# A three-stage float32 kernel (attention, then two expert layers) on one core: late attention's weights times values in unsplit float32, two heads side by side, with a new order of the work

## The chip, the core and the metric

The kernel runs on one core of a Trainium2 chip. The core has five engines that run side by side, each through its own list of instructions in order: TensorE (PE; its weight loads are shown as PEld), VectorE (DVE), ScalarE (ACT), GpSimd (POOL) and SyncE (SP), whose queue issues nearly all transfers. The metric is the device time of one execution in microseconds (us); lower is better.

## What is computed

The reference, cut to what matters:

```python
# attention: 4 batches, 8 heads, 576 positions, head size 64
scores = scale * np.matmul(q, k.transpose(0, 1, 3, 2))
bias = -(cum[:, :, :, None] - cum[:, :, None, :])       # cum: running sum of max(s, 0)
scores = np.where(causal, -1000000000.0, scores + np.minimum(bias, 0.0))
attn = np.exp(scores - np.max(scores, axis=-1, keepdims=True))
attn = attn / (np.sum(attn, axis=-1, keepdims=True) + 1e-09)
attn_out = np.matmul(attn, v)
x = attn_out.transpose(0, 2, 1, 3).reshape(2304, 512)
# two layers, each 512 -> 2048 -> 512
h = x @ moe_w_in;  x = (h * np.clip(h + 3.0, 0.0, 6.0) / 6.0) @ moe_w_out
h = x @ moe2_w_in; x = (h * np.tanh(softplus(h))) @ moe2_w_out
```

All tensors are float32, and the weights of the layers arrive as 64-bit words.

## The kernel before

**Attention** is cut into two kinds of work, each for a pair of heads. `small` (16 of them) does the first 256 query positions of a pair, `unit` (16) the other 320 against all 576 keys; the change's name "late attention" means the units. Each makes scores on PE, a masked sum with the row's extreme on DVE, the exponential on ACT, a normalisation, and PE transposes of the weights into PSUM banks, which are moved into a tile `pt`. Then PE multiplies weights and values (PV).

**float32 by parts.** A product that must keep float32's precision is made of float32r matmuls: each operand is split into a high part (a copy into float32r) and a low part (a subtraction on DVE), and three or four products of the parts are added in PSUM. `split` and the last steps of `load_split` are such splits. The small units' PV (L685) takes plain float32 operands instead, without parts, and puts one head's 64 output rows in the lower half of the PSUM bank and the other head's in the upper half. A unit's PV (L576) is split: `vt` holds the high and low part of v side by side, 128 columns for one head, `pt` holds both parts of the weights (L559 makes the low ones), each head has a bank `po` and ten matmuls, and the bank's two halves are added at L580 (ACT) and L582 (DVE) into a tile `x`, which is stored in DRAM as `xs`.

**The layers** go over five blocks of tokens (512, 512, 384, 512, 384), and in each block over 16 steps of 128 hidden columns. A step is a first product (L736, four groups of three matmuls, one group for each quarter of the inner dimension), a nonlinearity on ACT and DVE with a split into the tile `g` or `wo`, and a second product (L769 in the first layer, L774 in the second), which gathers in four banks over the 16 steps and is evicted by `y_out` (L792). The first layer's blocks 0 and 1 are written by the small units straight from PSUM (L695 writes the low part); blocks 2 to 4 are loaded from `xs` by `load_block` and split there. Block i's quarter c needs the heads 2c and 2c + 1 of all its batches.

**The order** is made by a list planner (`Plan.run`) while the program is built. Every piece of work has an engine or a choice of two, a guessed cost, a priority and the buffers it needs; the planner takes the ready piece of the lowest priority, and the resulting list of each engine is fixed. The priorities come from offsets in the table `T`. `la` and `la2` say by how many steps the first products go ahead of the second ones in the first and second layer. Buffers rotate in rings: `st`, from which x and y are stored, has four.

Of the kernel before, what the change touches and what calls it, by code (L numbers as in the profile page):

```python
# [34 lines left out]
    sm=4.004, sm2=3.667, w0=5.919, w1=9.193, cum=14.045, wo=0.795, blk0=27.645, blk1=17.49, wo2=40.913,  # L35
    wo2r=11.978, win2=5.088, g=29.605, upre=6.511, uhalf=0.883, upost=2.212, uv=0.304, spre=9.559, shalf=0.728,
    spost=1.761, pe=4.796, bias=2.278, la=1, la2=1, wp=5.083, p0=-8.796, p1=2.0, p2=2.856,
    p3=60.483, p4=83.372, p5=119.475, s0=31.523, s1=22.0, s2=23.277, s3=50.368, s4=66.006, s5=29.106,
# [207 lines left out]
def tile_attention_moe_moe(ctx, tc, qk1, qk, v1, s, w_in, w_out, w2_in, w2_out, out):  # L246
    nc = tc.nc

    def r(ap):
# [4 lines left out]
        "wo": 3, "qk": 2, "cb": 2, "nm": 2, "l": 2, "v": 1, "pt": 1, "qkr": 2,  # L254
# [22 lines left out]
    xs = [[dr.tile([P, n], F32, name=f"xs{i}_{c}") for c in range(NCC)] for i, (_, n) in enumerate(BLOCKS)]  # L277
# [18 lines left out]
    setup_b = Buf(dyn("att"), "pt", [P, 3 * S + CTOT], F32)  # L296

    def rows():
        room = setup_b.t[0:NB * NH]
        s_sb, one, cum = (room[:, S * i:S * (i + 1)] for i in range(3))  # L300
        return s_sb, one, cum, room[:, 3 * S:3 * S + CTOT]
# [121 lines left out]
    def unit(b, h, prio, step, dep0, depc, banks):  # L423
# [94 lines left out]
        pt = Buf(ap, "pt", [P, 2, 2, 1280], F32R)  # L518
        prev_t = None
        n_p = []  # L520
        for i in range(ta, tb):
# [9 lines left out]
            for g, cs in ([(0, (4, 3)), (0, (2, 1, 0))] if i == 4 else [(0, range(i, -1, -1)), (1, range(i, -1, -1))]):  # L531
# [9 lines left out]
                def views(ps, cs, i, g):  # L541
                    nch = len(cs)
                    if i == 4:
                        s_ = ps.t[:, 0:nch * P].rearrange("p (c g n) -> p c g n", g=2, n=D)
                        z0, st = (0, 4) if cs[0] == 4 else (9, 5)
                        d = [pt.t[:, k].rearrange("p g (c n) -> p c g n", n=D)[:, z0:z0 + st * (nch - 1) + 1:st] for k in range(2)]
                    else:
                        s_ = ps.t[:, 0:nch * P].rearrange("p (c n) -> p c n", n=P)
                        qo = P * i - q0
                        d = [pt.t[:, k, g].rearrange("p (c n) -> p c n", n=nq)[:, 4 - nch:, qo:qo + P] for k in range(2)]  # L550
                    return s_, d[0], d[1]
# [12 lines left out]
        x = Buf(main_p, "st", [P, 512], F32)  # L564
        n_x, n_pv = [], None
        for g in range(2):
            po = Bank(banks)
            hi, lo = (0, D) if g == 0 else (D, 0)

            def pv(po=po, g=g):  # L570
                for c in range(tb):
                    a = max(0, P * c - q0)
                    f = (3 - c) * nq + a if c < 4 else 0
                    w = vt.t[:, g, c].rearrange("p a d -> p (a d)")
                    for k in range(2):
# [366 lines left out]
```

## Time and profile before

| | us |
|---|---|
| median of 3 runs | 1014.72 (1013.29 to 1015.25) |
| the profiled execution | 1013.87 |
| its span | 1012.1 |
| PE busy | 992.1 |
| DVE busy | 541.8 |
| ACT busy | 496.0 |

The span runs from the first instruction's start to the last one's end; the execution's own time is 1.77 us longer. Busy times of PE overlap between neighbouring matmuls, so what a matmul takes of PE's time is read from its start to the next one's start. Attention's last matmul of a unit lies near 471 us; what follows is layers alone.

### The profile page before, as it was taken

What the parts mean: (1) busy time and instruction counts of PE and PEld (TensorE: products, weight loads), DVE (VectorE), ACT (ScalarE), POOL (GpSimd) and SP (SyncE); (2) the same over time, 40 slices, a digit from 0 to 9 for tenths busy, and PEclk for the clock granted to TensorE, in tenths of its full rate; (3) what the DMA queues carried; (4) which work ended last, traced back from release to release, by engine and by line L of the source; (5) the groups of instructions that cost most, each with busy time, mean ns of one, the idle gap of its engine ahead of it and who ended that gap; (6) DMA issues with size and microseconds to landing.
All of it is one profiled execution on the core that took longest, in us unless ns stands there. A gap on an engine that the chain in (4) does not pass through costs nothing.

```text
span 1012.1 us, 13938 instructions
## 1 busy us (share of the span) xinstructions
PE 992.1 (98%) x5016; PEld 826.6 (82%) x5016; DVE 541.8 (54%) x1213; ACT 496.0 (49%) x1046; POOL 45.0 (4%) x102
## 2 busy tenths in 40 slices
PE   6999999999999999999999999999999999999997
PEld 3557777778787898988889998888888888888896
DVE  6888988877767776774627888612112112111111
ACT  4878777756555666665326456423223223222222
POOL 2111101110010000000000000000000000000000
PEclk9889999999999999999999999999999999999999
DMA  6767857785565756543526775201001102000101
GB/s 215 231 211 259 287 190 246 227 284 178 171 186 169 238 176 197 177 123 137 207 104 237 261 266 201 86 1 53 22 1 42 42 1 63 0 1 1 42 1 32
DMA packets 56900, 140.81 MB, mean 139 GB/s; under 512 B 6944, under 2 KB 20288, under 8 KB 56832
## 3 DMA queue, kind: packets, MB, share of 16 engines
q1 hardware_dynamic: 56832, 139.93, 42.5%
q8 instruction: 40, 0.66, 0.3%
q14 instruction: 28, 0.23, 0.1%
HBM read 119.22 MB, written 20.68 MB: 138 GB/s over the span
## 4 chain that ended last, share of the span: by engine, by line
PE 89%; DVE 2%; DMA 2%; ACT 2%; issue 0%; DVEq 0%; ACTq 0%; SPq 0%
PE b L736 38%; PE b L774 20%; PE b L769 19%; PE b L492 4%; PE b L576 3%; PE b L538 3%; PE b L631 1%; DMA ys<-st 1%; PE b L685 1%; PE b L676 1%; DMA xs<-st 0%; ACT cb L527 0%; DVE pt L559 0%; DMA blk<-xs 0%; DMA cb<-cums 0%
## 5 line engine op out<-in xcount | busy, mean ns | idle before, releaser
L736 PE MATMUL b<-blk,win 128*128 128x512 f32 (+1 forms) x1920 | 504.4, 374 | 2.8 <-DVE e L749 1.2
L736 PEld LDWEIGHTS b<-blk,win 128*128 128x128 f32 x1920 | 348.9, 189 | 61.8 <-issue 5.7
L769 PE MATMUL b<-g,wo 128*128 128x512 f32 (+1 forms) x960 | 259.1, 380 | 0.1
L769 PEld LDWEIGHTS b<-g,wo 128*128 128x128 f32 x960 | 168.5, 188 | 27.8 <-issue 10.5
L757 DVE TENSOR_TENSOR g<-e,g 128x512 fp32r<-128x512 f32 (+1 forms) x120 | 76.6, 638 | 183.6 <-ACT g L290 183.0
L754 ACT ACTIVATE e<-b 128x512 f32<-128x512 f32 (+1 forms) x80 | 44.4, 555 | 254.2 <-PE b L736 253.5
L774 PE MATMUL b<-wo,g 128*128 128x512 f32 x432 | 122.1, 392 | 0.4 <-ACT g L290 0.4
L774 PE MATMUL b<-wo,wo 128*128 128x512 f32 x432 | 122.2, 391 | 0.0
L757 DVE TENSOR_TENSOR wo<-e,wo 128x512 fp32r<-128x512 f32 (+1 forms) x40 | 25.5, 638 | 136.1 <-ACT wo L290 136.1
L290 ACT ACTIVATE g<-e 128x512 fp32r<-128x512 f32 (+1 forms) x103 | 60.5, 587 | 65.6 <-PE b L769 52.5
L774 PEld LDWEIGHTS b<-wo,g 128*128 128x128 f32 x432 | 80.4, 188 | 13.9 <-ACT g L290 0.9
L774 PEld LDWEIGHTS b<-wo,wo 128*128 128x128 f32 x432 | 80.7, 188 | 12.7
L747 ACT ACTIVATE e<-b,three 128x512 f32<-128x512 f32 (+1 forms) x80 | 51.3, 642 | 34.8 <-PE b L736 22.4
L507 ACT ACTIVATE cb<-cb,nm 128x384 f32<-128x384 f32 (+2 forms) x80 | 54.5, 683 | 26.2 <-DVE nm L499 26.0
L559 DVE TENSOR_TENSOR pt<-b,pt 128x384 fp32r<-128x384 f32 (+2 forms) x96 | 54.6, 577 | 15.2 <-ACT pt L290 14.2
L749 DVE SCALAR_TENSOR_TENSOR e<-e,b 128x512 f32<-128x512 f32 (+1 forms) x80 | 50.4, 630 | 19.0 <-ACT e L747 18.6
L290 ACT ACTIVATE pt<-b 128x384 fp32r<-128x384 f32 (+2 forms) x96 | 48.1, 505 | 24.9 <-PE b L538 24.1
L499 DVE CUSTOM_DVE_ANT_0 cb<-b,cb 128x384 f32<-128x384 f32 (+2 forms) x80 | 44.7, 588 | 17.2 <-PE b L492 15.2
L538 PE MATMUL b<-ident,cb 128*128 128x128 f32 x304 | 48.7, 273 | 0.6 <-DVE pt L559 0.4
L538 PEld LDWEIGHTS b<-ident,cb 128*128 128x128 f32 x304 | 38.3, 140 | 12.2 <-issue 2.2
L576 PEld LDWEIGHTS b<-pt,v 128*128 128x128 f32 x320 | 46.8, 189 | 1.7
L492 PE MATMUL b<-qk 64*128 64x384 f32 (+2 forms) x288 | 46.5, 364 | 0.6 <-DVE pt L559 0.6
(83 smaller groups left out, 862.2 us busy)
## 6 DMA issues: line engine op xcount, KB each, us to landing
wo<-wos SPq DMA_DIRECT2D x64, 512.0 KB, 3.9
wraw<-in_w_in_dram SPq DMA_DIRECT2D x32, 512.0 KB, 4.4
wraw<-in_w_out_dram SPq DMA_DIRECT2D x32, 512.0 KB, 4.4
cb<-cuml SPq DMA_DIRECT2D x16, 896.0 KB, 7.0
wos<-wo SPq DMA_DIRECT2D x16, 512.0 KB, 5.7
qkr<-in_qk_dram SPq DMA_DIRECT2D x16, 480.0 KB, 3.8
qkr<-in_v_dram SPq DMA_DIRECT2D x16, 320.0 KB, 6.7
cb<-cums SPq DMA_DIRECT2D x12, 384.0 KB, 4.3
```

The costliest lines, as they stand in the source:

```text
L290: nc.scalar.activation(out=out_, in_=in_, func=AF.Copy)
L492: nc.tensor.matmul(out=ps[g].t[:, 0:w], lhsT=t.t[s_, ka, qo:qo + P], rhs=t.t[s_, kb, nk0 + a:nk0 + e], start=k == 0, stop=k == 2)
L507: nc.scalar.activation(out=p.t[:, o:o + w], in_=p.t[:, o:o + w], func=AF.Exp, scale=-1.0, bias=nm.t[:, k:k + 1], accum_out=l.t[:, k:k + 1],)
L538: nc.tensor.transpose(out=ps.t[:, P * z:P * (z + 1)], in_=p.t[:, o:o + P], identity=ident)
L559: nc.vector.tensor_tensor(out=dl, in0=s_, in1=r(dh), op=ALU.subtract)
L576: nc.tensor.matmul(out=po.t[:, a:nq], lhsT=w, rhs=pt.t[:, k, g, f:f + nq - a], start=c == 0 and k == 0, stop=c == tb - 1 and k == 1)
L736: nc.tensor.matmul(out=hps.t[:, 0:N], lhsT=w.t[:, a, P * c:P * (c + 1)], rhs=x.t[:, c, b, :], start=(c == 0 and k == 0), stop=(c == NCC - ...
L747: a = add("ACT", actp(N, 1), lambda: nc.scalar.activation(out=e0.t[:, 0:N], in_=hps.t[:, 0:N], func=AF.Relu, bias=three, scale=1.0), [prev ...
L749: a = add("DVE", v1x(N), lambda: nc.vector.scalar_tensor_tensor(out=e0.t[:, 0:N], in0=e0.t[:, 0:N], scalar=6.0, in1=hps.t[:, 0:N], op0=ALU ...
L757: gl = add("DVE", v1x(N), lambda: nc.vector.tensor_tensor(out=g.t[:, 1, 0:N], in0=src.t[:, 0:N], in1=r(g.t[:, 0, 0:N]), op=ALU.subtract), ...
L769: nc.tensor.matmul(out=y[j].t[:, 0:N], lhsT=wt.t[:, a, P * j:P * (j + 1)], rhs=g.t[:, b, 0:N], start=(f == 0 and k == 0), stop=(f == NF - ...
L774: nc.tensor.matmul(out=y[j].t, lhsT=g.t[:, a, P * j:P * (j + 1)], rhs=wt.t[:, b, :], start=(f == 0 and k == 0), stop=(f == NF - 1 and k == 2),
```

## The change

A unit's v is loaded as float32 into a tile of its own and not split. `pt` holds each weight once, as float32; L559 and its 96 subtractions are gone, and the eviction may go to ACT or DVE. PV becomes one group of ten float32 matmuls, over the five key chunks and in each over the two heads, whose outputs lie in the two halves of one bank. The output is split as it leaves that bank: a high part `xh` (copy) and a low part `xl` (subtraction on DVE), both stored, so that `xs` has two halves and `load_block` of the first layer loads them without a split. `v` and `pt` have two buffers each. All offsets of the order are new, `la` goes from 1 to 3 and `la2` from 1 to 2.

```diff
-    spost=1.761, pe=4.796, bias=2.278, la=1, la2=1, wp=5.083, p0=-8.796, p1=2.0, p2=2.856,
...
+    spost=1.158, pe=5.322, bias=2.302, la=3, la2=2, wp=11.079, p0=-8.796, p1=2.0, p2=2.856,
...
-        "wo": 3, "qk": 2, "cb": 2, "nm": 2, "l": 2, "v": 1, "pt": 1, "qkr": 2,
+        "wo": 3, "qk": 2, "cb": 2, "nm": 2, "l": 2, "v": 2, "pt": 2, "qkr": 2,
...
-    xs = [[dr.tile([P, n], F32, name=f"xs{i}_{c}") for c in range(NCC)] for i, (_, n) in enumerate(BLOCKS)]
+    xs = [[dr.tile([P, 2, n], F32, name=f"xs{i}_{c}") for c in range(NCC)] for i, (_, n) in enumerate(BLOCKS)]
...
-        vt = Buf(ap, "v", [P, 2, tb, 2, D], F32R)
-
-        def v_view(low):
-            return vt.t[:, :, :, low, :]
-        vr = Buf(ap, "qkr", [P, 2, tb, D], F32)
-        n_v0 = A("SP", 0.5, lambda: nc.sync.dma_start(
-            out=vr.t, in_=v1[b, h:h + 2].rearrange("g p c d -> p g c d")), dep0, prio, [vr], lat=dma(P * 2 * tb * D * 4))
-        n_v1 = A(("ACT", "DVE"), (act(2 * tb * D), v2x(2 * tb * D)), lambda e: copy(e, v_view(0), vr.t), [n_v0], prio + T["uv"] * step, [vt], [vr])
-        n_v2 = A("DVE", v1x(2 * tb * D), lambda: nc.vector.tensor_tensor(
-            out=v_view(1), in0=vr.t, in1=r(v_view(0)), op=ALU.subtract), [n_v1], prio + T["uv"] * step, (), [vt, vr])
+        vt = Buf(ap, "v", [P, 2, tb, D], F32)
+        n_v = A("SP", 0.5, lambda: nc.sync.dma_start(
+            out=vt.t, in_=v1[b, h:h + 2].rearrange("g p c d -> p g c d")), dep0, prio + T["uv"] * step, [vt], lat=dma(P * 2 * tb * D * 4))
...
-        pt = Buf(ap, "pt", [P, 2, 2, 1280], F32R)
+        pt = Buf(ap, "pt", [P, 2, 1280], F32)
...
-                def ev_h(ps=ps, cs=cs, i=i, g=g):
-                    s_, dh, _ = views(ps, cs, i, g)
-                    copy("ACT", dh, s_)
-
-                def ev_l(ps=ps, cs=cs, i=i, g=g):
-                    s_, dh, dl = views(ps, cs, i, g)
-                    nc.vector.tensor_tensor(out=dl, in0=s_, in1=r(dh), op=ALU.subtract)
-                n_ph = A("ACT", actp(nch * P), ev_h, [prev_t], half, (), [ps, pt])
-                n_pl = A("DVE", v1x(nch * P), ev_l, [n_ph], half, (), [ps, pt])
-                n_p += [n_ph, n_pl]
-
-        x = Buf(main_p, "st", [P, 512], F32)
-        n_x, n_pv = [], None
-        for g in range(2):
-            po = Bank(banks)
-            hi, lo = (0, D) if g == 0 else (D, 0)
-
-            def pv(po=po, g=g):
-                for c in range(tb):
-                    a = max(0, P * c - q0)
-                    f = (3 - c) * nq + a if c < 4 else 0
-                    w = vt.t[:, g, c].rearrange("p a d -> p (a d)")
-                    for k in range(2):
-                        nc.tensor.matmul(out=po.t[:, a:nq], lhsT=w, rhs=pt.t[:, k, g, f:f + nq - a],
-                                         start=c == 0 and k == 0, stop=c == tb - 1 and k == 1)
-            n_pv = A("PE", 0.2 + 2 * sum(mm_cost(nq - max(0, P * c - q0)) for c in range(tb)), pv, n_p + [n_v1, n_v2, n_pv], post,
-                     [po] if g else [po, x], [po, pt, vt])
-            n_b = A("ACT", actp(nq), lambda po=po, hi=hi, lo=lo: nc.scalar.activation(
-                out=x.t[hi:hi + D, 0:nq], in_=po.t[lo:lo + D, 0:nq], func=AF.Copy), [n_pv], post, (), [po, x])
-            n_x.append(A("DVE", v1x(nq), lambda po=po, hi=hi: nc.vector.tensor_tensor(
-                out=x.t[hi:hi + D, 0:nq], in0=po.t[hi:hi + D, 0:nq], in1=x.t[hi:hi + D, 0:nq], op=ALU.add),
-                [n_b], post, (), [po, x]))
+                        d = pt.t[:, g].rearrange("p (c n) -> p c n", n=nq)[:, 4 - nch:, qo:qo + P]
+                    copy(e, d, s_)
+                n_p.append(A(("ACT", "DVE"), (actp(nch * P), v1x(nch * P)), ev, [prev_t], half, (), [ps, pt]))
...
+        po = Bank(banks)
+        def pv():
+            for c in range(tb):
+                a = max(0, P * c - q0)
+                f = (3 - c) * nq + a if c < 4 else 0
+                for g in range(2):
+                    nc.tensor.matmul(out=po.t[D * g:D * (g + 1), a:nq], lhsT=vt.t[:, g, c, :], rhs=pt.t[:, g, f:f + nq - a],
+                                     start=c == 0, stop=c == tb - 1)
+        n_pv = A("PE", 0.1 + 0.00178 * sum(nq - max(0, P * c - q0) for c in range(tb)), pv, n_p + [n_v], post, [po], [pt, vt])
+        xh = Buf(main_p, "st", [P, 512], F32R)
+        xl = Buf(main_p, "st", [P, 512], F32R)
+        n_h2 = A(("ACT", "DVE"), (actp(nq), v1x(nq)), lambda e: copy(e, xh.t[:, 0:nq], po.t[:, 0:nq]), [n_pv], post, [xh], [po])
+        n_l2 = A("DVE", v1x(nq), lambda: nc.vector.tensor_tensor(
+            out=xl.t[:, 0:nq], in0=po.t[:, 0:nq], in1=r(xh.t[:, 0:nq]), op=ALU.subtract), [n_h2], post, [xl], [po, xh])
...
+                for k, (x, dep) in enumerate(((xh, n_h2), (xl, n_l2))):
+                    xs_n[i, h // 2].append(A("SP", 0.5, lambda i=i, a=a, e=e, b0=b0, k=k, x=x: nc.sync.dma_start(
+                        out=xs[i][h // 2][:, k, a - b0:e - b0], in_=r(x.t[:, a - t0:e - t0])),
+                        [dep], post, (), [x], lat=dma(P * (e - a) * 4)))
...
+            if layer == 0:
+                ld = add("SP", 0.5, lambda c=c: nc.sync.dma_start(out=r(t.t)[:, c], in_=xs[i][c][:]),
...
+            if layer == 0:
+                blk_n[layer, i, c] = [ld]
+                continue
```

In the changed kernel the lines have other numbers: L736 is L722, L769 is L755, L774 is L760, L576 is L555, L685 is L664, L695 is L674, L364 is L365.

On PE, the first unit's PV. `b6` and `b7` are PSUM banks, and the last size is what one matmul moves. Before:

```order
L769 MATMUL b3_947<-g_1045,wo_1156 128x512 x3
L736 MATMUL b5_1175<-blk_147,win_680 128x512 x3
L576 MATMUL b6_1246<-pt_1115,v_986 128x320 x6
L576 MATMUL b6_1246<-pt_1115,v_986 128x192 x2
L576 MATMUL b6_1246<-pt_1115,v_986 128x64 x2
L676 MATMUL b7_1263<-ident_69,cb_966 128x128 x3
L769 MATMUL b0_885<-g_1188,wo_1218 128x512 x3
L736 MATMUL b5_1175<-blk_147,win_680 128x512 x3
L576 MATMUL b7_1292<-pt_1115,v_986 128x320 x6
L576 MATMUL b7_1292<-pt_1115,v_986 128x192 x2
```

And of the change:

```order
L755 MATMUL b2_921<-g_1046,wo_1140 128x512 x3
L655 MATMUL b6_1218<-ident_69,cb_985 128x128 x3
L755 MATMUL b3_936<-g_1046,wo_1140 128x512 x3
L655 MATMUL b7_1229<-ident_69,cb_985 128x128 x3
L555 MATMUL b6_1235<-pt_1135,v_170 64x320 x6
L555 MATMUL b6_1235<-pt_1135,v_170 64x192 x2
L555 MATMUL b6_1235<-pt_1135,v_170 64x64 x2
```

Two groups in two banks, a head each, have become one group in one bank.

On PE, the end of the program. Before (`b4` is a first product's bank, `b0` to `b2` the second product's):

```order
L736 MATMUL b4_8875<-blk_7948,win_6469 128x384 x3
L774 MATMUL b2_8533<-wo2_6691,g_8855 128x512 x3
L736 MATMUL b4_8875<-blk_7948,win_6469 128x384 x3
L774 MATMUL b0_8512<-wo2_6717,wo_8879 128x512 x3
L736 MATMUL b4_8875<-blk_7948,win_6469 128x384 x3
L774 MATMUL b1_8525<-wo2_6717,wo_8879 128x512 x3
L736 MATMUL b4_8875<-blk_7948,win_6469 128x384 x3
L774 MATMUL b2_8533<-wo2_6717,wo_8879 128x512 x3
L774 MATMUL b0_8512<-wo2_6749,g_8905 128x512 x3
L774 MATMUL b1_8525<-wo2_6749,g_8905 128x512 x3
L774 MATMUL b2_8533<-wo2_6749,g_8905 128x512 x3
```

And of the change:

```order
L722 MATMUL b5_8543<-blk_7616,win_6155 128x384 x9
L760 MATMUL b0_8174<-wo2_6396,wo_8547 128x512 x3
L722 MATMUL b5_8543<-blk_7616,win_6155 128x384 x3
L760 MATMUL b1_8182<-wo2_6396,wo_8547 128x512 x3
L760 MATMUL b2_8194<-wo2_6396,wo_8547 128x512 x3
L760 MATMUL b0_8174<-wo2_6423,g_8570 128x512 x3
L760 MATMUL b1_8182<-wo2_6423,g_8570 128x512 x3
L760 MATMUL b2_8194<-wo2_6423,g_8570 128x512 x3
```

Between the last first product (L736, now L722) and the second product that needs it (reading the last `g`) one group of three stood before, and two stand now.

On DVE, where the eighth pair of small units writes its low part into block 0, the last that the block waits for. `win` is a finished weight split, `wtmp` one that is being made. Before:

```order
L643 ISA cb,nm<-b_642,cb 128x256
L643 ISA nm 128x1
L364 TENSOR_TENSOR win<-wtmp,win 128x512
L344 TENSOR_SCALAR wtmp<-wtmp 128x512
L643 ISA cb,nm<-b_687,cb 128x128
L643 ISA nm 128x1
L348 SCALAR_TENSOR_TENSOR wtmp<-wraw,wtmp 128x512
L695 TENSOR_TENSOR blk<-b_674,blk 128x256
L354 SCALAR_TENSOR_TENSOR wtmp<-wraw,wtmp 128x512
```

And of the change:

```order
L674 TENSOR_TENSOR blk<-b_651,blk 128x256
L622 ISA cb,nm<-b_679,cb 128x128
L622 ISA nm 128x1
L365 TENSOR_TENSOR win<-wtmp,win 128x512
L345 TENSOR_SCALAR wtmp<-wtmp 128x512
L622 ISA cb,nm<-b_679,cb 128x256
L622 ISA nm 128x1
L349 SCALAR_TENSOR_TENSOR wtmp<-wraw,wtmp 128x512
L674 TENSOR_TENSOR blk<-b_688,blk 128x256
L355 SCALAR_TENSOR_TENSOR wtmp<-wraw,wtmp 128x512
```

The `win` row in the first piece is the eighth weight's, that in the second the ninth's.

## Rows read from the trace of the kernel before

**Rows 1.** The page: the span; busy us of the engines; granted PE clock in 40 slices, tenths.

```profile
span 1012.1 us, 13938 instructions
...
PE 992.1 (98%) x5016; PEld 826.6 (82%) x5016; DVE 541.8 (54%) x1213; ACT 496.0 (49%) x1046; POOL 45.0 (4%) x102
```

**Rows 2.** Windows: length, busy us (instructions) of PE, PEld, DVE, ACT, POOL; clock; DMA.

```profile
0.00:75.00 75.00, 62.63 (x271) 38.17 (x271) 59.56 (x199) 53.47 (x160) 12.95 (x28) 0.91 0.69 219
75.00:475.00 400.00, 397.56 (x2237) 327.80 (x2238) 302.86 (x708) 264.17 (x577) 32.08 (x74) 1.00 0.64 201
```

**Rows 3.** Waits of PE, 75 to 1010 us: in total, times, the longest.

```profile
PE b L736 <- DVE e L749: 1.2, 2, 0.8
PE b L492 <- DVE pt L559: 0.6, 1, 0.6
PE b L774 <- ACT g L290: 0.4, 1, 0.4
PE b L538 <- DVE pt L559: 0.4, 2, 0.2
```

**Rows 4.** Timeline of PE at 387 us: start, us, line, count [idle before].

```profile
387.49 1.40 PE L576 MATMUL b<-pt,v 128*128 128x320 f32 x10
388.73 0.77 PE L736 MATMUL b<-blk,win 128*128 128x384 f32 x3
```

**Rows 5.** Timeline of PE at 125 us.

```profile
124.86 0.86 PE L736 MATMUL b<-blk,win 128*128 128x512 f32 x3
125.56 0.84 PE L769 MATMUL b<-g,wo 128*128 128x512 f32 x3
126.34 0.88 PE L685 MATMUL b<-qk 128*64 128x256 f32 x8
127.14 0.98 PE L769 MATMUL b<-g,wo 128*128 128x512 f32 x3
```

**Rows 6.** Line L685: duration in ns, min/median/max; first and last start; forms.

```profile
L685 PEld LDWEIGHTS b<-qk x128: 132/137/232, 20.9 to 197.7; 128*64 128x64 f32 x128
L685 PE MATMUL b<-qk x128: 272/379/689, 20.9 to 197.8; 128*64 128x256 f32 x64, 128*64 128x128 f32 x64
```

**Rows 7.** Groups of DVE, 75 to 475 us: count, busy us, mean ns, idle before.

```profile
L559 DVE TENSOR_TENSOR pt<-b,pt 128x384 fp32r<-128x384 f32 (+2 forms) x96 | 54.6, 577 | 15.2 <-ACT pt L290 14.2
...
L348 DVE SCALAR_TENSOR_TENSOR wtmp<-wraw,wtmp 128x512 uint32<-128x512 uint32 x20 | 13.8, 692 | 0.1
...
L364 DVE TENSOR_TENSOR wo<-wtmp,wo 128x512 fp32r<-128x512 f32 x15 | 10.5, 699 | 0.3
L344 DVE TENSOR_SCALAR wtmp<-wtmp 128x512 uint32<-128x512 uint32 x20 | 8.5, 423 | 1.1 <-ACT wtmp L338 0.8
```

**Rows 8.** Timeline of PE, block 0's last quarter, and its first second product.

```profile
56.63 0.49 PE L736 MATMUL b<-blk,win 128*128 128x512 f32 x1 [0.72 <-ACT blk L290]
57.51 0.73 PE L736 MATMUL b<-blk,win 128*128 128x512 f32 x2 [0.39 <-DVE blk L695]
...
75.70 0.86 PE L769 MATMUL b<-g,wo 128*128 128x512 f32 x3
```

**Rows 9.** Windows of 12 and of 4 us, columns as in rows 2.

```profile
56.00:68.00 12.00, 10.98 (x36) 6.97 (x38) 10.33 (x33) 8.52 (x26) 1.31 (x2) 0.72 0.62 208
60.00:64.00 4.00, 4.00 (x10) 2.41 (x10) 3.96 (x15) 2.76 (x8) 0.00 (x0) 0.50 0.35 123
```

**Rows 10.** Timeline of PE, its last two entries.

```profile
1003.62 0.86 PE L774 MATMUL b<-wo,wo 128*128 128x512 f32 x3
1004.91 2.47 PE L774 MATMUL b<-wo,g 128*128 128x512 f32 x9 [0.44 <-ACT g L290]
```

**Rows 11.** Timeline of DVE at 140 us.

```profile
140.36 1.02 DVE L559 TENSOR_TENSOR pt<-b,pt 128x384 fp32r<-128x384 f32 x2
...
142.22 0.68 DVE L749 SCALAR_TENSOR_TENSOR e<-e,b 128x512 f32<-128x512 f32 x1
```

**Rows 12.** The chain that ended last, at 341 us: start, us, what.

```profile
341.40 8.24 DMA ys<-st
```

More of the change, by code (lines that the diff above doesn't have):

```diff
@@ L34 @@
 T = dict(
[L35 to L38 removed]
+    sm=3.895, sm2=5.532, w0=5.919, w1=9.308, cum=14.045, wo=0.564, blk0=27.645, blk1=12.97, wo2=44.236,
+    wo2r=11.978, win2=5.088, g=30.578, upre=6.511, uhalf=1.145, upost=3.306, uv=0.304, spre=6.035, shalf=0.728,
+    spost=1.158, pe=5.322, bias=2.302, la=3, la2=2, wp=11.079, p0=-8.796, p1=2.0, p2=2.856,
+    p3=65.354, p4=87.114, p5=119.475, s0=30.881, s1=22.0, s2=23.277, s3=36.84, s4=66.006, s5=29.106,
 )
@@ L294, in copy @@
             nc.vector.tensor_copy(out=out_, in_=in_)
-    setup_b = Buf(dyn("att"), "pt", [P, 3 * S + CTOT], F32)
+    setup_a = Buf(dyn("att"), "pt", [P, 3 * S], F32)
+    setup_b = Buf(dyn("att"), "pt", [P, CTOT], F32)
     def rows():
-        room = setup_b.t[0:NB * NH]
+        room = setup_a.t[0:NB * NH]
         s_sb, one, cum = (room[:, S * i:S * (i + 1)] for i in range(3))
-        return s_sb, one, cum, room[:, 3 * S:3 * S + CTOT]
+        return s_sb, one, cum, setup_b.t[0:NB * NH]
     def setup_load():
@@ L539, in unit, with ev @@
                 prev_t = A("PE", nch * P * 0.0008475, tr, [n_n[g], prev_t], half, [ps] if prev_t else [ps, pt], [p])
-                def views(ps, cs, i, g):
+                def ev(e, ps=ps, cs=cs, i=i, g=g):
                     nch = len(cs)
@@ L545, in views @@
                         z0, st = (0, 4) if cs[0] == 4 else (9, 5)
-                        d = [pt.t[:, k].rearrange("p g (c n) -> p c g n", n=D)[:, z0:z0 + st * (nch - 1) + 1:st] for k in range(2)]
+                        d = pt.t.rearrange("p g (c n) -> p c g n", n=D)[:, z0:z0 + st * (nch - 1) + 1:st]
                     else:
@@ L716, in load_block @@
         for c in range(NCC):
-            ld = add("SP", 0.5, lambda c=c: nc.sync.dma_start(out=r(t.t)[:, c, 1, :], in_=(xs, ys)[layer][i][c][:]),
-                     src_n[i, c] + ([first] if c else []), prio, [t] if c == 0 else [], [t], lat=dma(P * n * 4))
+            if layer == 0:
+                ld = add("SP", 0.5, lambda c=c: nc.sync.dma_start(out=r(t.t)[:, c], in_=xs[i][c][:]),
+                         src_n[i, c] + ([first] if c else []), prio, [t] if c == 0 else [], [t], lat=dma(P * n * 8))
+            else:
+                ld = add("SP", 0.5, lambda c=c: nc.sync.dma_start(out=r(t.t)[:, c, 1, :], in_=ys[i][c][:]),
+                         src_n[i, c] + ([first] if c else []), prio, [t] if c == 0 else [], [t], lat=dma(P * n * 4))
             if c == 0:
                 first = ld
+            if layer == 0:
+                blk_n[layer, i, c] = [ld]
+                continue
             blk_n[layer, i, c] = split(ld, prio, t, (lambda c=c: t.t[:, c, 0, :], lambda c=c: t.t[:, c, 1, :]), n)
@@ L821, in tile_attention_moe_moe @@
         PRO = -100
-        n_b = add("X", 0.0, lambda: None, [n0], -1e6, [setup_b])
-        n_s = add("SP", 0.475, setup_load, [n_b], -1e6, (), [setup_b], lat=dma(NB * NH * S * 4))
+        n_a = add("X", 0.0, lambda: None, [n0], -1e6, [setup_a])
+        n_b = add("X", 0.0, lambda: None, [n_a], -1e6, [setup_b])
+        n_s = add("SP", 0.475, setup_load, [n_b], -1e6, (), [setup_a], lat=dma(NB * NH * S * 4))
         n_id = add("POOL", 1.2, setup_const, [n0], -1e6)
-        n_one = add("DVE", 0.5, setup_one, [n_b], -1e6, (), [setup_b])
-        n_c1 = add("DVE", 1.3, lambda: setup_cum(0, 256, (0, 1)), [n_s, n_one], -1e6, (), [setup_b])
-        n_c2 = add("DVE", 2.6, lambda: setup_cum(256, S, (2, 3, 4)), [n_c1], PRO + T["cum"], (), [setup_b])
+        n_one = add("DVE", 0.5, setup_one, [n_b], -1e6, (), [setup_a])
+        n_c1 = add("DVE", 1.3, lambda: setup_cum(0, 256, (0, 1)), [n_s, n_one], -1e6, (), [setup_a, setup_b])
+        n_c2 = add("DVE", 2.6, lambda: setup_cum(256, S, (2, 3, 4)), [n_c1], PRO + T["cum"], (), [setup_a, setup_b])
         nc0s = add("SP", 0.475, lambda: nc.sync.dma_start(out=cums[:, 0:384], in_=rows()[3][:, 0:384]), [n_c1], -1e5, (), [setup_b],
```

5 lines of the change are left out of this document (removed).

## The prediction

> **What bounds the kernel now.** I read the page first: PE is busy 98% of a span of 1012.1 us [rows 1]. Matmul ends are modelled, so that share alone proves little, and I went on to the windows and the waits. From 75 to 475 us, while attention and the first layer share the core, PE is busy 397.6 of 400 us and DVE 302.9 [rows 2]. In the table of waits PE idles after 75 us for 2.6 us in all, four entries, three of them released by DVE [rows 3]. In the first 75 us DVE is busy 59.6 us, and PE waits for the end of chains PE, DVE, ACT, DVE, PE [rows 2, 8], with stretches at half the granted clock behind such gaps [rows 9]. So the end comes when PE has issued its work: what counts is how much time PE's instructions take from start to start, how late PE becomes saturated, and the few waits behind that. Work taken off DVE and ACT after 75 us is worth what it takes out of those waits, and no more.
>
> **The PV matmuls.** There are 16 big units (4 batches, 4 head pairs), each with two groups of ten float32r matmuls. One group takes 388.73 - 387.49 = 1.24 us from its first start to the next instruction's [rows 4]; a unit takes 2.48 us. The change makes of them one group of ten float32 matmuls in the same columns: 320 three times, 192 and 64, which is 1216 columns a head, with the two heads in the two halves of the array's columns. The trace of before has no such group of that size, but it has the form itself: the small units' PV at L685, four float32 matmuls of 256 and 128 columns for two heads. It shows as eight instructions, so a float32 matmul is two. The whole takes 127.14 - 126.34 = 0.80 us [rows 5]. Durations are 272 ns at the least, which are the 128 wide ones, and 379 in the median, 256 wide [rows 6]: 107 ns for 128 columns, or 0.836 ns a column and instruction. For one head, 384 columns times two instructions make 0.64 us; for two heads one after the other they would make 1.28. The group takes 0.80, so the heads run side by side, and 0.16 us are fixed.
>
> For 1216 columns: 2 x 0.836 x 1216 = 2.03 us, plus the fixed 0.16, plus what the 64 wide pieces need over their columns. L685's weight loads take 137 ns in the median [rows 6], and two of them must fit beside a piece of 53 ns; I add 0.07. Going into such a group costs too: three matmuls of 512 take 125.56 - 124.86 = 0.70 us ahead of others of their kind and 126.34 - 125.56 = 0.78 ahead of L685 [rows 5], so 0.09 with rounding. Sum 2.35 us, against 2.48. The gain is 0.13 x 16 = **2.1 us**. The bounds: if the whole of L685's 0.80 us scaled with its 384 columns, a unit would take 2.53 + 0.09 and the kernel would lose 2.3 us; if only the columns counted, 2.03, it would gain 7.2. I stay near the middle, because the two durations in rows 6 separate columns from the fixed part.
>
> The trace shows a price of 0.09 us on the way in, and the fixed 0.16 holds what the way out costs. [...]
>
> **DVE and ACT.** The 96 subtractions at L559 (54.6 us) go [rows 7], and with them the 16 at L469, the v casts, half of the output's steps and the splits of the three loaded blocks. Of the evictions into pt that stay, 95 of 96 stand on ACT, where they stood. All of it lies after 75 us, beside a PE that is busy 397.6 of 400 us, so directly it is worth nothing. Indirectly: of the waits in rows 3, 1.0 us is for L559 itself, and the 1.2 us for L749 has its larger part at 142.2 us, where two L559, 1.02 us together, stand just ahead of L749 on DVE [rows 11]. I count these 2.2 us as gone, and give 1.2 back for waits that the new order brings and that I can't see; the nearest row is a store of y that took 8.24 us to land [rows 12]. Term: **1.0 us** gained, bounds 2.2 gained and 2 lost.
>
> **The end.** Before, the last step's second product has 0.69 us of other matmuls ahead of it after the last first product. PE goes on at 1004.91, where 1003.62 + 0.69 = 1004.31 was possible [rows 10]: 0.60 us lost, waiting for ACT and DVE to make g. In the new order two such groups of three stand in between, 1.38 us, and the chain from the last first product to g, from 1003.62 to 1004.91, took 1.29. Term: **0.6 us** gained, bounds 0 and 0.6.
>
> **The beginning.** Nothing is removed here; the order alone moves. Block 0's last quarter waits for the eighth pair of small units: PE waits 0.72 us at 56.63 for ACT and 0.39 at 57.51 for DVE [rows 8]. On DVE eight weight splits stand ahead of that pair's last write before, and nine after. A split has four DVE instructions of 0.42 + 2 x 0.69 + 0.70 = 2.5 us [rows 7]. If DVE were full, the quarter would come 2.5 us later, at about 59; but the weight is then ready earlier, and when PE comes to its first second product (75.70 before), DVE has done the same work in both orders: eleven splits of w_in, one of w_out, the same pairs. DVE has 15.4 idle us in those 75 [rows 2] in which the early split may lie. Also, SP's queue now has two v loads of 320 KB early, ahead of the store of the sums on which every later pair's mask depends. I take **0**, bounds 2.5 gained and 6 lost (2.5 for the split, and one more stretch at half clock, which by the 0.72 over 12 us in rows 9 lasts 2 x 0.28 x 12 = 6.7 us and loses at most half of them).
>
> **Queues.** SP issues 24 more stores of x and loads blocks of double size. Its queue has rows to spare, and the loads no longer end in a cast and a subtraction. Costed at nothing: the cover is PE's other work between a unit's PV and the block's first use, which I count as some 12 us at the tightest place (block 2, last quarter). Without that cover it would cost up to 2 us there, which is inside the wait term's bound.
>
> **The sum.** 1013.87 us of the profiled execution (its span 1012.1 and 1.8 around it) - 2.1 - 1.0 - 0.6 + 0 = 1010.2. The median of the runs shown, 1014.72, lies 0.85 above that execution, so I predict **1011.0**.
>
> **Rivals.** First, the early part eats the gain: block 0 comes a split later and the late PE never gets it back. For it: PE waits exactly there now [rows 8]. Against: the idle DVE time. 1011.0 + 2.5 = 1013.5, with some scatter 1012.7 to 1016.7, no change. Second, on the other side, the clock: the later quarter leaves PE idle long enough for another stretch like that from 58 to 65 us, where the granted clock is 0.50 in the window from 60 to 64 [rows 9]. It costs 2.5 + 3.4 = 5.9 us, 1016.9; it decides for slower from 5.7 us on. For it: PE fell back right behind the waits of rows 8. Against: in the new order PE's first first-product stands five rows earlier, so that some work lies where PE waits now. Third, the two heads don't run side by side: the second head's 2.03 us come on top, 16 x 2.03 = 32.5, so 1043.5. L685 speaks against it, which has the same form in an order less favourable, both matmuls of one head first. [...] Fourth, a better case: the early split lies wholly in idle time and the pairs move up, and 1008.5 or less follows.
>
> **How the numbers follow.** A measurement of this kernel can tell about 0.2%, 2 us. The forecast (1007 to 1012.7) has 0.54, the fourth rival's tail below 1007 0.05, the first 0.25, the second 0.13, the third 0.03. Faster is the forecast and the fourth, 0.59; same 0.25; slower 0.16. The range 1006 to 1017 leaves out the third rival, most of the second's upper half and the tail below, together under 0.2; the forecast's own range is 1007 to 1012.7.
>
> **What would show it.** In the profile after, the new PV group should take 2.25 to 2.45 us from its first start to the next instruction's, with 20 instructions in pairs; twice that is the third rival. PE's waits after 75 us should have no entry from an eviction into pt, and under 2 us in all. The last group of nine at L760 should have no wait ahead of it. The first second product should start between 70 and 76 us. The windows of the first 75 us should show two stretches at half clock; three mean the second rival. The prediction is wrong if PE's first saturated window comes over 3 us later than now, or if ACT waits for a store of x or y at about 340 us for so long that PE stands.

## The result, and the profile after

The changed kernel takes 1002.96 us in the median (1000.74 to 1003.14, 4 runs), beside 1014.93 for the kernel before (1013.29 to 1015.25, 4 runs). The ratio is 0.988, with a 95% interval of 0.9863 to 0.9898: 12.0 us, 1.2%, faster. The forecast was 1011.0, with a range from 1006 to 1017. The sign was right, and the gain is three times the one that was worked out.

The page of the changed kernel, its span and the busy time of its engines (they answer to [rows 1]):

```profile
span 1001.4 us, 13786 instructions
...
PE 982.1 (98%) x5016; PEld 803.8 (80%) x5016; DVE 462.4 (46%) x1067; ACT 476.9 (48%) x1008; POOL 44.1 (4%) x102
```

Its windows, columns as in [rows 2], the first two answering to those, the last to [rows 9]:

```profile
0.00:75.00 75.00, 60.80 (x278) 37.67 (x280) 61.34 (x206) 55.19 (x167) 10.62 (x28) 0.89 0.75 243
75.00:475.00 400.00, 399.73 (x2276) 314.05 (x2273) 234.51 (x579) 249.55 (x542) 33.45 (x74) 1.00 0.70 222
24.00:40.00 16.00, 14.74 (x62) 9.03 (x63) 11.22 (x40) 12.31 (x40) 1.54 (x4) 0.51 0.57 191
56.00:68.00 12.00, 11.94 (x61) 7.68 (x56) 11.53 (x40) 10.48 (x32) 1.25 (x2) 1.00 0.81 262
```

DVE's busy time from 75 to 475 us fell from 302.9 to 234.5, and PE's idle time there from 2.4 us to 0.3. The granted clock was 0.51 from 24 to 40 us, and 1.00 where it had been 0.50 before, from 60 to 64.

The waits of PE from 75 us on, as in [rows 3]; of the four entries before none is left:

```profile
PE b L722 <- DMA blk<-xs: 0.3, 1, 0.3
```

The timeline of PE round one unit's PV, which answers to [rows 4]:

```profile
203.11 0.86 PE L722 MATMUL b<-blk,win 128*128 128x512 f32 x3
203.90 2.27 PE L555 MATMUL b<-pt,v 128*64 128x320 f32 x20
206.10 0.96 PE L755 MATMUL b<-g,wo 128*128 128x512 f32 x3
206.90 0.40 PE L722 MATMUL b<-blk,win 128*128 128x512 f32 x1
```

The whole unit takes 206.10 - 203.90 = 2.20 us, where two groups of 1.24 stood. The groups of three on either side take 0.79 and 0.80, where [rows 5] has 0.70 ahead of the same kind.

The end, which answers to [rows 10], and the first second product, which stood at 75.70 before:

```profile
69.70 1.63 PE L755 MATMUL b<-g,wo 128*128 128x512 f32 x6
...
992.83 1.55 PE L760 MATMUL b<-wo,wo 128*128 128x512 f32 x6
994.22 2.36 PE L760 MATMUL b<-wo,g 128*128 128x512 f32 x9
```

**Where the time came from.** Both kernels issue 5016 matmuls, and only PV's differ. So I took from each trace, for every matmul, the time from its start to the next one's. PV's are summed as they are. From the others their columns are taken off, at the rate that they have where PE is saturated (0.443 ns a column in the layers and the scores, 0.844 in the transposes, 0.42 in the small units' PV, 0.66 to 1.0 in their other matmuls); what is left is waits, slow clock and the price of going from one kind to another. The rates are the same for all kernels, so the differences hang little on them. In us, with a second profiled execution of the changed kernel (the run called changed_again below):

| | before | changed | changed again | forecast of the gain |
|---|---|---|---|---|
| left over until 75 us | 39.6 | 38.0 | 36.2 | 0 |
| PV, 16 units | 40.1 | 35.1 | 35.1 | 2.1 |
| left over from 75 to 480 us | 14.6 | 11.0 | 10.2 | 1.0 |
| left over from 480 to 980 us | 5.1 | 5.5 | 5.3 | 0 |
| left over behind 980 us | 6.6 | 5.7 | 5.6 | 0.6 |
| span | 1012.1 | 1001.4 | 998.5 | 3.7 |

Between the first two columns the gain is 1012.1 - 1001.4 = 10.7 us, which is 1.6 + 5.0 + 3.6 - 0.4 + 0.9. The forecast's terms make 3.7.

### The profile page after: what moved, and what is told of

Its sections match the earlier page's. It is cut to its first block, busy times and chain, and to the rows that moved or that the text cites. A ratio compares the mean times of both kernels' runs of the same rounds, so it can differ in the third digit from the quotient of the medians.

```text
span 1001.4 us, 13786 instructions
## 1 busy us (share of the span) xinstructions
PE 982.1 (98%) x5016; PEld 803.8 (80%) x5016; DVE 462.4 (46%) x1067; ACT 476.9 (48%) x1008; POOL 44.1 (4%) x102
## 4 chain that ended last, share of the span: by engine, by line
PE 95%; DVE 2%; DMA 1%; ACT 1%; issue 0%; SPq 0%; DVEq 0%; ACTq 0%
PE b L722 40%; PE b L755 20%; PE b L760 20%; PE b L486 4%; PE b L555 4%; PE b L532 3%; PE b L610 2%; PE b L664 1%; PE b L655 1%; DMA xs<-st 1%; DMA blk<-xs 0%; PE b L613 0%; DVE g L622 0%; DMA pt<-in_s_dram 0%; DVE win L365 0%
## 5 line engine op out<-in xcount | busy, mean ns | idle before, releaser
L722 PE MATMUL b<-blk,win 128*128 128x512 f32 (+1 forms) x1920 | 505.5, 373 | 0.3 <-DMA blk<-xs 0.3
L722 PEld LDWEIGHTS b<-blk,win 128*128 128x128 f32 x1920 | 347.0, 188 | 58.6 <-issue 6.6
L755 PE MATMUL b<-g,wo 128*128 128x512 f32 (+1 forms) x960 | 258.7, 378 | 0.0
L755 PEld LDWEIGHTS b<-g,wo 128*128 128x128 f32 x960 | 170.3, 188 | 28.6 <-issue 8.4
L760 PE MATMUL b<-wo,wo 128*128 128x512 f32 x432 | 122.1, 391 | 0.0
L760 PE MATMUL b<-wo,g 128*128 128x512 f32 x432 | 122.0, 391 | 0.0
L760 PEld LDWEIGHTS b<-wo,g 128*128 128x128 f32 x432 | 80.5, 188 | 13.3 <-DVE g L743 0.3
L760 PEld LDWEIGHTS b<-wo,wo 128*128 128x128 f32 x432 | 80.6, 188 | 12.9
L290 ACT ACTIVATE pt<-b 128x384 f32<-128x384 f32 (+2 forms) x95 | 48.0, 505 | 19.8 <-PE b L532 18.8
L532 PE MATMUL b<-ident,cb 128*128 128x128 f32 x304 | 48.8, 272 | 0.0
L532 PEld LDWEIGHTS b<-ident,cb 128*128 128x128 f32 x304 | 39.0, 140 | 9.2 <-ACT cb L521 0.2
L355 DVE SCALAR_TENSOR_TENSOR wtmp<-wraw,wtmp 128x512 uint32<-128x512 uint32 x64 | 44.2, 691 | 1.0
L349 DVE SCALAR_TENSOR_TENSOR wtmp<-wraw,wtmp 128x512 uint32<-128x512 uint32 x64 | 44.1, 690 | 1.2
```

Source lines behind the costliest of these rows:

```text
L290: nc.scalar.activation(out=out_, in_=in_, func=AF.Copy)
L532: nc.tensor.transpose(out=ps.t[:, P * z:P * (z + 1)], in_=p.t[:, o:o + P], identity=ident)
L722: nc.tensor.matmul(out=hps.t[:, 0:N], lhsT=w.t[:, a, P * c:P * (c + 1)], rhs=x.t[:, c, b, :], start=(c == 0 and k == 0), stop=(c == NCC - ...
L755: nc.tensor.matmul(out=y[j].t[:, 0:N], lhsT=wt.t[:, a, P * j:P * (j + 1)], rhs=g.t[:, b, 0:N], start=(f == 0 and k == 0), stop=(f == NF - ...
L760: nc.tensor.matmul(out=y[j].t, lhsT=g.t[:, a, P * j:P * (j + 1)], rhs=wt.t[:, b, :], start=(f == 0 and k == 0), stop=(f == NF - 1 and k == 2),
```

## The experiments

In new_code_old_order, old_code_new_order and extra_sub the two theories differ on the waits in the middle: that the work which left DVE ended them (theory 1), or that the new offsets did (theory 2). Times are medians; the kernel before, run beside the experiments on three chips, took 1014.3 (12 runs), 1014.3 (15 runs) and 1013.9 us (7 runs).

**The code without the offsets: new_code_old_order**

```diff
-    sm=3.895, sm2=5.532, ..., pe=5.322, bias=2.302, la=3, la2=2, wp=11.079, ...
+    sm=4.004, sm2=3.667, ..., pe=4.796, bias=2.278, la=1, la2=1, wp=5.083, ...
```

> The changed kernel with all offsets of the table T, la and la2 as they were before. Theory 1 (the work that left DVE ended the waits of PE in the middle, and the new offsets bring only the beginning and the last wait): the gain over the kernel before is that of PV, 5.1 us, and of the waits from 140 to 460 us, 3.8, so about 1006.0, and the wait of 0.6 us ahead of the last group is back. Theory 2 (the new offsets ended those waits, less work on DVE is worth nothing): the gain is PV's alone, 5.1, so about 1009.8, and PE's waits from 75 us on come to some 4 us.

1005.0 us (1004.3 to 1005.4), ratio 0.9903 (0.9888 to 0.9919). Nine of the twelve us come with the code, and this is nearer theory 1. Left over from 75 to 480 us are 12.0, against 14.6 before and 11.0 with the new offsets; until 75 us 38.9. The wait ahead of the last group is back, as theory 1 said. PE's waits:

```profile
PE b L760 <- ACT g L290: 0.4, 1, 0.4
PE b L532 <- DVE nm L622: 0.3, 1, 0.3
PE b L486 <- DVE nm L493: 0.2, 1, 0.2
PE b L532 <- ACT pt L290: 0.2, 1, 0.2
```

**The offsets without the code: old_code_new_order**

```diff
-    sm=4.004, sm2=3.667, ..., pe=4.796, bias=2.278, la=1, la2=1, wp=5.083, ...
+    sm=3.895, sm2=5.532, ..., pe=5.322, bias=2.302, la=3, la2=2, wp=11.079, ...
```

> The kernel before with all offsets of the changed one. Theory 1: only the beginning (1.4 us) and the last wait (0.6) are gained, about 1012.9, and PE still waits some 4 us between 140 and 460 us for evictions into pt and what stands behind them. Theory 2: 1.4 + 0.6 + 3.8 = 5.8 are gained, about 1009.1, and those waits are gone.

1028.1 us (1027.9 to 1029.2), ratio 1.0135 (1.0121 to 1.0149): slower by 13.8, which neither theory had. From 75 to 480 us 27.9 us are left over, and PV has 3.4 more in it than before. The view puts 12.2 us of waits down; its three largest of nine entries, of which the first has no releaser that the profile shows and the second is for the low parts of the weights (L559):

```profile
PE b L538 <- issue: 3.8, 2, 2.8
PE b L538 <- DVE pt L559: 3.3, 2, 2.3
PE b L492 <- DVE st L582: 1.3, 1, 1.3
```

So the two halves of the change can't be added: alone they are worth -9.3 and +13.8 us, together -12.0.

**The order of the heads: heads_outer**

```diff
-            for c in range(tb):
...
-                for g in range(2):
+            for g in range(2):
+                for c in range(tb):
...
                     nc.tensor.matmul(out=po.t[D * g:D * (g + 1), a:nq], ...
```

> The changed kernel with the ten matmuls of a unit's PV in another order, all five of one head first, then all five of the other; everything else stands where it stood. Theory 1 (each half of the array's columns goes through its own matmuls, so that the heads run side by side in either order, as the small units' PV suggests): the group takes 2.2 us as before, 1003.0 within 1. Theory 2 (only neighbours in the list run side by side): the group takes about 2 x 2.03 + 0.16 = 4.2 us, 16 x 2.0 = 32 more, 1035.

1029.5 us (1027.9 to 1029.9), ratio 1.0143 (1.0128 to 1.0158). Theory 1 fell. The timeline of PE round a unit's PV:

```profile
207.78 3.94 PE L555 MATMUL b<-pt,v 128*64 128x320 f32 x20
211.66 0.73 PE L755 MATMUL b<-g,wo 128*128 128x512 f32 x2
```

3.88 us, 1.68 more than the changed kernel's 2.20, and 16 x 1.68 = 26.9 is what the run lost (26.5). This prices the heads' running side by side in this kernel: without most of it the change would have made it slower. The instructions of this group that started before 209.455 us, by form (busy us, mean ns):

```profile
L555 PE MATMUL b<-pt,v 128*64 128x320 f32 x6 | 1.8, 441 | 0.0
...
L555 PE MATMUL b<-pt,v 128*64 128x192 f32 x1 | 0.3, 326 | 0.0
```

These are seven of the first head's ten instructions. In the trace's starts the second head's first one comes at 209.457 us, ahead of the first head's last three, at 209.614, 209.776 and 209.832. So it isn't the neighbours alone that run side by side: three instructions stood between.

**Blocks of four instructions: heads_by_two**

```diff
-            for c in range(tb):
...
-                for g in range(2):
+            for c, g in ((0, 0), (1, 0), (0, 1), (1, 1), (2, 0), (3, 0), (2, 1), (3, 1), (4, 0), (4, 1)):
```

> The changed kernel with a unit's PV in blocks of two matmuls (four instructions) of one head, then two of the other, and so on. Theory 1 (a matmul of the other half starts while up to three instructions of the first half that stand ahead of it still wait, as the trace of heads_outer shows at the border and the small units' PV shows in blocks of four): the group stays near 2.2 us, 1003.0 within 1. Theory 2 (only direct neighbours in the list run side by side): each of the four borders saves one of 0.27 us from 4.06 + 0.16, so about 3.1 us a group, 16 x 0.9 = 15 us more, 1018.

1002.85 us (1002.0 to 1003.8), beside 1002.39 for the changed kernel on the same chip. Theory 1 holds:

```profile
202.90 2.33 PE L554 MATMUL b<-pt,v 128*64 128x320 f32 x20
205.16 0.96 PE L754 MATMUL b<-g,wo 128*128 128x512 f32 x3
```

2.26 us, against 3.88 in heads_outer. Four instructions of one head and then four of the other run side by side, ten and ten only at their border. That is why the small units' PV at L685, with four and four, showed two heads in the time of one (0.80 us [rows 5]).

**The subtractions back on DVE: extra_sub and extra_max**

```diff
                     copy(e, d, s_)
+                    nc.vector.tensor_tensor(out=s_, in0=s_, in1=d, op=ALU.subtract)   # extra_sub
+                    nc.vector.tensor_tensor(out=d, in0=d, in1=d, op=ALU.max)          # extra_max
```

(one of the two lines in each kernel)

> The changed kernel with 96 subtractions put back on DVE, each right behind its eviction into pt, where the old ones stood; they write over the bank that they read, and nothing uses what they write. PE's list is word for word that of the changed kernel. Theory 1 (the work that left DVE ended the waits): PE's waits from 100 to 475 us come back to some 3 to 4 us, 1006 to 1007. Theory 2 (the order ended them): within 0.5 of 1003.0.

> As extra_sub, but the 96 instructions put back on DVE read and write only the weights in pt (each the maximum of a value with itself, in place), so that they keep DVE busy at the same places without holding the bank that a later transpose waits for; PE's list is that of the changed kernel. Theory 1 (what the subtractions cost is the bank that they hold longer): the transposes no longer wait, 1003 to 1005. Theory 2 (what they cost is DVE's time, which everything behind them on DVE waits for): 1013 to 1017, near extra_sub's 1017.3.

extra_sub took 1017.3 us (1016.6 to 1017.9), 14.4 more than the changed kernel and four times what theory 1 said. extra_max took 1010.9 (1009.5 to 1011.5), 7.9 more, between its theories. The added instructions are alike, 56.1 and 54.7 us in all; DVE's groups from 75 to 475 us, first of extra_sub, then of extra_max:

```profile
L546 DVE TENSOR_TENSOR b<-b,pt 128x384 f32<-128x384 f32 (+2 forms) x96 | 56.1, 586 | 33.2 <-ACT pt L290 32.6
```

```profile
L546 DVE TENSOR_TENSOR pt<-pt 128x384 f32<-128x384 f32 (+2 forms) x96 | 54.7, 578 | 29.2 <-ACT pt L290 28.6
```

PE's waits, the three largest of six entries each, first of extra_sub, then of extra_max:

```profile
PE b L532 <- DVE b L546: 3.0, 8, 1.2
PE b L532 <- issue: 1.1, 3, 0.4
PE b L656 <- issue: 0.9, 1, 0.9
```

```profile
PE b L556 <- DVE pt L546: 2.2, 3, 1.0
PE b L532 <- ACT pt L290: 1.1, 1, 1.1
PE b L532 <- DVE st L562: 0.6, 1, 0.6
```

In extra_sub it is the transposes (L532) that wait, for banks that the subtraction still reads; in extra_max PV itself waits for pt. So in this fixed order both count. The 7.9 us are the price of the load together with pt's later readiness. The 6.5 us between the two runs are not the price of the bank alone, because extra_sub doesn't make PV wait for pt as extra_max does.

**The same load, planned: old_order_subs_planned and new_order_subs_planned**

```diff
-                n_p.append(A(("ACT", "DVE"), (actp(nch * P), v1x(nch * P)), ev, [prev_t], half, (), [ps, pt]))
+                n_ph = A("ACT", actp(nch * P), lambda ev=ev: ev("ACT"), [prev_t], half, (), [ps, pt])
+                n_p += [n_ph, A("DVE", v1x(nch * P), sub, [n_ph], half, (), [ps, pt])]
```

(`sub` is extra_sub's line; the first kernel has the old offsets too)

> The changed kernel with the old offsets and with the 96 subtractions as planned work on DVE (evictions on ACT, each subtraction holds the bank, nothing uses its output): PV's change alone, in an order made for that load. Theory 1 (with an order that knows of it, the load of the subtractions is worth what the waits of the kernel before show, 3.8 us): 1005.0 + 3.8 = 1008.8, PV alone 5.5 of the 12 us. Theory 2 (their load is worth nothing where the order knows of it): 1005.0.

> The same planned subtractions under the new offsets. Theory 1 (the new offsets pack attention so that DVE must have been relieved, as the old code's 13.8 us loss under them suggests): slower than the same code under the old offsets, 1010 to 1017. Theory 2 (an order made with the load in view is as good under either offsets): 1005 to 1009.

1006.5 us (1004.4 to 1006.7) under the old offsets, 1.5 more than the same code without the subtractions, between the theories and nearer the second; the ranges of the two just overlap, and they ran on different chips. Left over from 75 to 480 us are 13.5, against 12.0 without, again 1.5. Under the new offsets 1012.3 (1011.7 to 1014.4), as theory 1 there had it. Its longest wait of PE is of another kind:

```profile
PE b L735 <- DMA blk<-xs: 6.1, 1, 6.1
```

The last units come so late that the first product of the next block waits 6.1 us for the block's load from `xs`. This one wait is as large as the whole difference from the old offsets, 5.8 us. So theory 1 had the time, but PE does not lose it to DVE directly; whether DVE's load is what makes the units late isn't shown.

**The small units' heads: small_heads_inner, and once more beside the changed kernel**

```diff
-            for g in range(2):
-                for c, a in ((0, 0), (1, P)):
+            for c, a in ((0, 0), (1, P)):
+                for g in range(2):
                     nc.tensor.matmul(out=po.t[D * g:D * (g + 1), a:N], ...
```

> The changed kernel with the small units' PV in the order of the large ones, chunk by chunk and in each both heads, nothing else moved. Theory 1 (with four matmuls of one head first, the second head starts late where PE's list is not far ahead, in the first 75 us above all): up to 0.4 us for some of the 8 pairs there, 1001.5 to 1003. Theory 2 (with four of a head the two run side by side already, and waits for DVE and ACT set the beginning): within 0.5 of 1003.0.

> The changed kernel once more, beside the two others of this call on the same chip: 1003.0 within 1.

> The small units' PV with the heads inner once more, beside the changed kernel. Theory 1 (it shortens the beginning, 1.1 us of the profile's 2.3): 1 to 2 us under the changed kernel of this call. Theory 2 (the first comparison lay within scatter): within 0.7 of it.

1001.5 us (1000.9 to 1002.1), against the 1002.96 of the result; then 1001.0 (1000.5 to 1002.5), beside 1002.4 (1000.3 to 1003.4) for the changed kernel on the same chip. Both comparisons come out 1.4 us better, and in both the ranges overlap. The two profiled executions of either kernel don't settle it: left over until 75 us are 36.9 and 38.2 with the heads inner, 38.0 and 36.2 without. Whether it helps stays open; it is the fastest version that was run, by less than its scatter.

The changed kernel's second profiled execution is 2.9 us shorter than its first, with the same instructions. Until about 33 us the two are 0.2 us apart; behind 42 us they are 2.0 to 2.2 apart. In between, the granted clock differs. From 33 to 40 us, and the starts of the same two groups, in the first execution:

```profile
33.00:40.00 7.00, 6.06 (x30) 3.80 (x28) 4.80 (x21) 5.71 (x20) 0.77 (x2) 0.52 0.70 225
```

```profile
30.92 1.66 PE L610 MATMUL b<-qkr 64*128 64x128 f32 x8
...
82.64 0.96 PE L722 MATMUL b<-blk,win 128*128 128x512 f32 x3
```

In the second:

```profile
33.00:40.00 7.00, 5.71 (x43) 3.84 (x40) 6.86 (x32) 6.94 (x27) 0.77 (x2) 1.00 0.76 261
```

```profile
30.74 1.66 PE L610 MATMUL b<-qkr 64*128 64x128 f32 x8
...
80.62 0.96 PE L722 MATMUL b<-blk,win 128*128 128x512 f32 x3
```

The first falls back by 2.02 - 0.18 = 1.84 us. So in one program some 7 us at a granted clock of 0.52 instead of 1.00 cost some 1.8 us here.

## Why the prediction was wrong

**The PV matmuls: mechanism right, size too small.** The heads run side by side (2.20 us a unit, 3.88 in heads_outer), and the form of L685 carried over. The step that failed is "Sum 2.35 us, against 2.48". 2.03 + 0.16 = 2.19 was already the answer; PV's 35.1 us are 2.19 a unit. The 0.07 for the 64 wide pieces isn't there: in the changed kernel the start of one pair of them is 0.055 us from the next pair's, 0.86 ns a column, where the others take 0.84. The 0.09 on the way in exists (0.79 against 0.70 in the timeline above), but it lies in the time of the group ahead. What the way out costs isn't in the fixed 0.16 either, as the prediction had it, but in the group behind (0.80). And the old kernel paid too, which the prediction left out. On PE around the old groups of [rows 4]:

```profile
386.97 0.68 PE L769 MATMUL b<-g,wo 128*128 128x384 f32 x3
...
389.33 1.40 PE L576 MATMUL b<-pt,v 128*128 128x320 f32 x10
```

The group ahead takes 387.49 - 386.97 = 0.52 us and the one behind 389.33 - 388.73 = 0.60: nothing on the way in, 0.08 on the way out, twice a unit. So in and out cost some 0.17 us a unit before and 0.2 now, and the 0.09 was nearly paid for. The old groups took 40.1 / 32 = 1.25 each, not 1.24. Term: 5.0 us, not 2.1.

The price on the way in is new: the group ahead of PV takes 0.79 us instead of 0.70, while the group ahead of the old PV, which used all 128 columns, took 0.52, as did the one before it (386.45 to 386.97). The 0.1 us on the way out can't be put down to the halves of 64 columns alone, because 0.08 of it stood behind the old groups as well.

**L685 as a witness.** The prediction called the order of L685, one head's matmuls first, "less favourable", and used it against the third rival. That held, because the changed kernel alternates. But what L685 shows goes for its four instructions and not for ten: heads_outer cost 26.5 us, near the 32.5 that the third rival was priced at. By the starts in heads_outer's trace, the second head's first matmul started ahead of three of the first head's that stood before it in the list (209.457 us against 209.614, 209.776 and 209.832), and behind the other seven. So over ten the order decides, and over four it does not (2.26 us a unit in heads_by_two).

**The waits: the view was read as if it were the loss.** "PE idles after 75 us for 2.6 us in all" was the step that failed. The view counts from the modelled end of the matmul before. The timeline of the kernel before at one of those waits, listed with 0.6 us:

```profile
384.07 0.44 PE L492 MATMUL b<-qk 64*128 64x384 f32 x1
385.10 0.80 PE L492 MATMUL b<-qk 64*128 64x384 f32 x5 [0.58 <-DVE pt L559]
385.82 0.44 PE L769 MATMUL b<-g,wo 128*128 128x384 f32 x1
```

From 384.07 to 385.82 the six matmuls take 1.75 us. The changed kernel has the same group without a wait:

```profile
330.87 0.80 PE L486 MATMUL b<-qk 64*128 64x384 f32 x6
331.59 0.97 PE L755 MATMUL b<-g,wo 128*128 128x512 f32 x3
```

0.72 us. So this wait cost 1.03, not 0.58. Shorter ones don't show in the view at all; in the kernel before, at 419 us, a group of three takes 0.91 us to the next start, and [rows 4] and the lines beside it have 0.52 for the same:

```profile
419.18 0.77 PE L769 MATMUL b<-g,wo 128*128 128x384 f32 x3
420.09 0.63 PE L538 MATMUL b<-ident,cb 128*128 128x128 f32 x4
```

extra_sub says the same at a larger scale: the view lists 6.1 us of waits in six entries, and the kernel lost 14.4. The gain there was 3.6 us (4.4 in the second execution) where the view of before lists 2.2, and the 1.2 us given back "for waits that the new order brings" did not come (one of 0.3 us for a load).

Who ended them is settled in part. The 96 subtractions, in an order that is made with them, are worth some 1.5 us (old_order_subs_planned against new_code_old_order, whose ranges overlap), not the 3.8 of theory 1. The new offsets bring 1.0 (12.0 to 11.0). The last 1.1 us lies in what else the code changes (PV's wait for the low parts, which the planned subtractions don't bring back, the splits of v, the output's steps, second buffers of v and pt); this is what remains of a subtraction, and no run takes these apart. Two executions of the changed kernel differ by 0.8 in this row, so none of the three shares is sharp.

**The end: right.** Two groups of three stand between, 994.22 - 992.83 = 1.39 us, and there is no wait. The left-over behind 980 us fell by 0.9 against 0.6. It comes with the order that offsets and code make together. Under the old offsets new_code_old_order has the wait of 0.4 as [rows 10] has it, but old_order_subs_planned has two groups and no wait; under the new ones the changed kernel has none, but new_order_subs_planned has it again. The last two entries of old_order_subs_planned, then of new_order_subs_planned:

```profile
995.55 1.55 PE L773 MATMUL b<-wo,wo 128*128 128x512 f32 x6
996.94 2.40 PE L773 MATMUL b<-wo,g 128*128 128x512 f32 x9
```

```profile
1001.73 0.86 PE L773 MATMUL b<-wo,wo 128*128 128x512 f32 x3
1003.02 2.48 PE L773 MATMUL b<-wo,g 128*128 128x512 f32 x9 [0.44 <-ACT g L290]
```

It isn't `la2`: with that alone put back to 1 in the changed kernel, the lists of all engines stay the same.

**The beginning: sign missed.** "I take 0" failed; 1.6 us were gained in one execution and 3.4 in the other. The ninth split ahead of the eighth pair cost nothing that can be seen. The first second product starts at 69.70 instead of 75.70, but most of that is its place in PE's list: 256 matmuls stand ahead of it where 273 did, and the 257th matmul started at 71.44 before.

The gain isn't one stretch of half clock less. Before, the granted clock was 0.50 from 60 to 64 us, while PE was busy all the time [rows 9], and in the changed kernel it is 1.00 there. But it is 1.00 from 58 to 66 us in new_code_old_order and old_order_subs_planned too, and they have 38.9 and 39.3 us left over. The second rival expected a third stretch; the changed kernel has one, from about 23 to 40 us (0.51 from 24 to 40), which is longer than the two of before together (0.57 from 34 to 42 and 0.57 from 58 to 66). Over the first 75 us the clock is 0.91 before [rows 2] and 0.89 in the changed kernel's first execution, which has 1.6 us less left over all the same.

The offsets bring at least part of it. At a clock of 0.89 over the first 75 us, the two profiled executions with the new code and the old offsets have the 38.9 and 39.3, and the four with the new offsets 38.0 to 38.3: some 1 us. By which waits is not shown. The rest goes with the clock of the execution: with the new code and offsets and 0.93 or 0.95 there, 36.2 to 37.7 are left over. The rival's price, at most 3.4 us for a stretch of 6.7, was a bound that held: the two executions above differ by some 7 us at half clock and part by 1.8.

**The range.** The terms missed 7.0 us of the profiled 10.7: PV 2.9, the waits 2.6, the beginning 1.6, the end 0.3, less 0.4 from 480 to 980. The range left out what happened because the waits' bound was drawn from the 2.6 us of the view, and because PV, the waits and the beginning all came out on the better side. PV and the beginning stayed inside their own bounds (7.2 and 2.5) in the first execution; the waits, 3.6 against 2.2, did not.

## What to carry to other kernels

Read what a wait costs from one start to the next, beside the same group without a wait; the view of waits, which counts from modelled ends, gave about half here. In these runs two halves of TensorE's columns ran side by side where their matmuls alternated within four instructions (2.20 and 2.26 us a unit), and mostly not with ten and ten (3.88), so write the loop over heads innermost. A table that orders the work belongs to the code that it was made for: the same offsets were worth 2 us with this code and cost 14 with the old one.

## What the runs showed of the hardware that was not expected

In heads_outer a float32 matmul into one half of the columns started ahead of three others for the other half that stood before it in the list (209.457 us against 209.614, 209.776 and 209.832); with ten of one half first, it waited until seven had started. In the changed kernel a pair of such matmuls of 320 columns, one in each half, took 0.269 us from one pair's start to the next, 0.84 ns a column, the same as one head alone: six pairs of 320 and one of 192 took 1.83 us to the next pair's start (203.90 to 205.73), and in heads_outer, where the second head began only at 209.457, the first head's six of 320 and one of 192 took 209.614 - 207.78 = 1.83. The group of three matmuls behind PV took longer than others (0.80 us instead of 0.70), also where PV used all 128 columns (0.60 instead of 0.52). And one program's executions differ by 2.0 us by the 75th microsecond, with granted clocks of 0.52 and 1.00 from 33 to 40 us: how long the clock stayed low there wasn't fixed by the program.
